# Loading two of six chunk rows with three large transfers in a one-core RWKV-and-MLP kernel

## The chip, the cores and the metric

The kernel runs on one core of one Trainium2 chip. The metric is the device time in microseconds of one execution. A core has TensorE (PE in the profile; PEld is its weight load), VectorE (DVE), ScalarE (ACT), GpSimd (POOL) and SyncE (SP), each with an instruction queue of its own that is worked off in order, and 16 DMA engines that carry out transfers which SP or ACT issue (SPq, ACTq).

## What is computed

The inputs r, k and v are fp32 of shape batch 4, heads 8, sequence 768, head width 48. A linear recurrence over the sequence is followed by a layer norm without offset and a two-layer MLP with a residual:

```python
for t in range(S):
    cur = np.einsum('bhd,bhe->bhde', u[None] * kt, vt)
    y[:, :, t] = np.einsum('bhd,bhde->bhe', rt, state + cur)
    state = w[None, :, :, None] * state + np.einsum('bhd,bhe->bhde', kt, vt)
...
xn = (x - mu) / np.sqrt(var + 1e-06) * g_ln      # x: (4, 768, 384), the heads side by side
ch = np.maximum(xn @ w_ch1, 0.0) @ w_ch2         # 384 -> 1536 -> 384
return (x + ch).astype(np.float32)
```

## The kernel before

The sequence is cut into six chunks of 128 tokens. With four batches that makes 24 tiles; tile i is chunk i // 4 of batch i % 4, with the 128 tokens on the partitions and 8 x 48 values along each partition. "Chunk rows 3 and 6" of the change are chunks 2 and 5 when counted from zero: tiles 8 to 11 and 20 to 23.

A tile goes through these steps, each a small function that a plan calls by a short name:

- LR, LK and LV (L325, L322, L328) load r, k and v of the tile, 192 KiB each, by a DMA that SP issues. One row of such a load is 48 fp32 values, 192 bytes.
- SR and SK (L334, L331) scale r and k by powers of the decay into the bf16 tile sc, through the helper of L194. CV (L337) casts v to bf16 (vv), through the helper copy of L187 to L191.
- r and k are turned so that the head width lies on the partitions: for the first eight tiles by PE (TR, TCr, TCk, TC), from tile 8 on by TKR (L489), a DMA transpose from sc to trs that SP issues.
- AT (L359) multiplies turned k and r, AM (L387) masks the product in PSUM into A, Q (L356) and S (L390) make the current-token term and the state update, CC copies the former to cc, ZU and ZD update the state Z, VB (L426) multiplies v by cc, Y (L432) multiplies by the state and by v, and X (L451) adds both into x.
- SQ and RS make the norm's factor, XN (L463) centres x into xn, and LT, LT2 or LTD turn it into xT. LT2 (L482) is a DMA transpose for two tiles at a time, issued by SP.
- UP (L511) multiplies xT by the first weight matrix into the PSUM pool hp, which has two buffers; RL (L528) applies the relu into hT and so frees the buffer; DN (L540) multiplies by the second matrix; OT (L602) adds the residual, and STO (L609) stores the tile.

The order of everything is written out by hand. PLAN (L18 to L67) is a list of steps "name,index,engine" with v for DVE, s for ACT, g for POOL; the loop of L619 calls them in that order, and each engine's queue, SP's too, gets its instructions in the order in which the plan names them. All r, k and v loads, all DMA transposes, the six weight loads and most stores are in SP's one queue. The stretch of the plan that matters for the prediction has LR,8 at the end of its line 31, and then these lines of the file:

```
32: Y,5,- CC,5,s RL,64,s DN,8,- LK,8,- AM,6,v VB,5,g TR,7,- RS,2,g LK,9,- UP,65,- UP,66,- Q,6,v TC,7,s X,5,v ZU,5,v DN,9,-
33: CV,7,g LV,8,- RL,66,s CV,6,g AT,7,- SQ,3,s RS,4,g XN,5,v LV,9,- Q,7,v S,6,- SR,8,v LT,5,- LR,10,- DN,10,- ZU,6,v SK,8,g
34: CC,6,s SQ,5,s RL,65,s XT,5,v Y,6,- STO,0,s AM,7,v S,7,- UP,81,- VB,6,g TKR,8,- LK,10,- SK,9,g OT,2,v UP,80,- CC,7,v X,6,v
35: SR,9,g DN,16,- RL,80,v XN,6,s Y,7,- CV,8,s RS,5,g DN,17,- VB,7,v TKR,9,- RL,81,s STO,1,- X,7,v CV,9,g DN,18,- ZU,7,v SQ,7,s
36: XN,7,g UP,82,- OT,4,v Q,8,g LT2,6,- AT,8,- RL,82,s DN,20,- LK,11,- AM,8,v LR,11,- SK,10,g S,8,- DN,21,- CC,8,s RS,3,g Y,8,-
```

Loaded tiles live in rings (L118 to L125): kf, rf and vf have 11 buffers each, and a load into a buffer waits until the readers of the tile 11 places earlier are done. Beside that, an SP transfer waits for the landing of the one eight places before it on the same completion counter, so about eight are under way at most.

Of the kernel before, what the change touches and what calls it, by code (L numbers as in the profile page):

```python
# [7 lines left out]
FP32 = mybir.dt.float32  # L8
# [5 lines left out]
GROUPS = [1, 1, 1, 1, 1, 1, 2, 2, 2, 2, 2, 2, 2, 1, 1, 1, 1]  # L14
ZPE = [4, 5, 6, 7]
K_BY_DMA = [8, 9, 10, 11, 12, 13, 14, 15, 16, 17, 18, 19, 20, 21, 22, 23]
SLOTS = {'kf': 11, 'rf': 11, 'vf': 11, 'sc': 3, 'vv': 4, 'trs': 3, 'q': 2, 'A': 2, 'cc': 4, 'Z': 6, 'ZS': 2, 'Vb': 3, 'x': 13, 'xn': 4, 'xT': 4, 'hT': 4, 'ot': 4}
PLAN = """  # L18
MP,0,v LR,1,- WF,0,s MW,0,v MI,0,g LR,0,- MM,0,g TL,0,s LC,1,- LK,0,- LV,0,- LN,0,s FR,0,s LC,0,s LR,2,- LK,1,- LC,2,s
SR,0,v FK,0,s SK,0,v LK,3,- DU,40,- CT,0,- TR,0,- CV,0,v LK,2,- SR,1,v TCr,0,s CP,0,v TCk,0,v UW,0,g LV,1,- UGC,0,s WL,0,s  # L20
# [50 lines left out]
def kernel(  # L71
# [12 lines left out]
    nc = tc.nc  # L84
    P = nc.NUM_PARTITIONS
    B, H, S, D = r.shape
    C = H * D
    L = P
    NCH = S // L
    NT = B * NCH  # L90
# [12 lines left out]
    const = ctx.enter_context(tc.tile_pool(name="const", bufs=1))  # L103
# [14 lines left out]
    def ring(name, shape, dtype):  # L118
        n = SLOTS[name]
        tiles = [const.tile(shape, dtype, name=f"{name}{a}") for a in range(n)]  # L120
        return lambda i: tiles[i % n]

    kf = ring("kf", [P, H, D], FP32)
    rf = ring("rf", [P, H, D], FP32)
    vf = ring("vf", [P, H, D], FP32)  # L125
    sc = ring("sc", [P, 2, H, DP], BF16)
    vv = ring("vv", [P, H, D], BF16)
    trs = ring("trs", [P, 2, HP, P], BF16)
    qq = ring("q", [P, HP, P], BF16)
    AA = ring("A", [P, 2, HP, P], BF16)  # L130
    cc = ring("cc", [P, H], FP32)
    ZZ = ring("Z", [P, HP, E2], BF16)
    ZS = ring("ZS", [P, HP, E2], FP32)
    Vb = ring("Vb", [P, C], FP32)
    xx = ring("x", [P, C], FP32)
    xn2 = [const.tile([P, 2, C], BF16, name=f"xn{a}") for a in range(SLOTS["xn"] // 2)]
    xT = ring("xT", [P, GM, CK, P], BF16)
    hT = ring("hT", [P, FK, GM * P], BF16)
    ot2 = [const.tile([P, 2, C], FP32, name=f"ot{a}") for a in range(SLOTS["ot"] // 2)]

    def scr(i):
        return sc(i)[:, 0]

    def sck(i):
        return sc(i)[:, 1]
# [17 lines left out]
    Fr = const.tile([P, H, D], FP32, name="Fr")  # L163
    Fk = const.tile([P, H, D], FP32, name="Fk")
# [3 lines left out]
    rows = const.tile([NR, P], FP32, name="rows")  # L168
# [18 lines left out]
    def copy(e, out, in_):  # L187
        if e == "s":
            nc.scalar.copy(out=out, in_=in_)  # L189
        else:  # L190
            engines[e].tensor_copy(out=out, in_=in_)  # L191

    def times(e, out, in0, in1):
        engines[e].tensor_tensor(out=out, in0=in0, in1=in1, op=ALU.mult)  # L194
# [4 lines left out]
    def chunk_src(t, i):  # L199
        c, b = divmod(i, B)  # L200
        return t[b, :, c * L : (c + 1) * L, :].rearrange("h t d -> t h d")
# [47 lines left out]
    def MP(i, e):  # L249
        for a in range(SLOTS["sc"]):  # L250
            nc.vector.memset(sc(a)[:, :, :, D:DP], 0.0)
        nc.vector.memset(WLZ[:], 0.0)
        nc.vector.memset(uwI[:], 0.0)
        nc.vector.memset(expo[:], -0.5)
# [56 lines left out]
    def w2_f(n):  # L311
        return w1_f[n][:].rearrange("p k f -> p (k f)").rearrange("p (a c) -> p a c", c=C)
# [4 lines left out]
    def CW(i, e):  # L317
        n, a = divmod(i, 2)
        h = FK // NW // 2
        copy(e, w2_sb[n][:, a * h : (a + 1) * h, :], w2_f(n)[:, a * h : (a + 1) * h, :])  # L320

    def LK(i, e):  # L322
        nc.sync.dma_start(out=kf(i)[:], in_=chunk_src(k, i))  # L323

    def LR(i, e):  # L325
        nc.sync.dma_start(out=rf(i)[:], in_=chunk_src(r, i))  # L326

    def LV(i, e):  # L328
        nc.sync.dma_start(out=vf(i)[:], in_=chunk_src(v, i))  # L329

    def SK(i, e):  # L331
        times(e, sck(i)[:, :, :D], kf(i)[:], Fk[:])

    def SR(i, e):  # L334
        times(e, scr(i)[:, :, :D], rf(i)[:], Fr[:])

    def CV(i, e):  # L337
        copy(e, vv(i)[:], vf(i)[:])

    def TR(i, e):  # L340
        t = psum["tr", i] = ps.tile([P, 2 * HP, P], BF16, name="tr")
# [83 lines left out]

    def VB(i, e):  # L426
        engines[e].tensor_tensor(  # L427
            out=Vb(i)[:].rearrange("p (h d) -> p h d", h=H), in0=vf(i)[:],
            in1=cc(i)[:].unsqueeze(2).to_broadcast([P, H, D]), op=ALU.mult,
        )  # L430

# [177 lines left out]
    def STO(i, e):  # L609
# [3 lines left out]
    steps = dict(  # L613
        WF=WF, LC=LC, CT=CT, CP=CP, LT2=LT2, TKR=TKR, DU=DU, MW=MW, TL=TL, MI=MI, MM=MM, MP=MP, WU=WU, LN=LN, FK=FK_, FR=FR_, UGC=UGC,
        UW=UW, WL=WL, LW1=LW1, SW=SW, LW2=LW2, CW=CW, LK=LK, LR=LR, LV=LV, SK=SK, SR=SR, CV=CV, TR=TR, TCr=TCr,
        TCk=TCk, TC=TC, Q=Q, AT=AT, AMa=AMa, AMb=AMb, AM=AM, S=S_, CC=CC, ZU=ZU, ZD=ZD, VB=VB, Y=Y, X=X,
        SQ=SQ, XN=XN, RS=RS, LT=LT, LTD=LTD, TKD=TKD, TRD=TRD, XT=XT, UP=UP, RL=RL, DN=DN, OT=OT, STO=STO, DA=DA, DB=DB, OA=OA, OB=OB, SA=SA, SB=SB,
    )
    for step in PLAN.split():  # L619
        name, i, e = step.split(",")  # L620
# [31 lines left out]
```

## Time and profile before

| what | value |
|---|---|
| median of three runs (lowest to highest) | 156.37 us (155.73 to 157.08) |
| span of the profiled execution | 156.2 us; what lies around it is taken as the 0.15 us to the median |
| PE busy | 139.4 us (89%) |
| DVE, ACT, POOL busy | 112.9, 75.1, 87.9 us (72%, 48%, 56%) |
| DMA packets, bytes | 104465, 30.03 MB |
| granted PE clock | 1.00 in every stretch |

The page gives, for one profiled execution, the busy time of each engine, the span in 40 equal slices (a digit is the busy share in tenths), the DMA queues, the chain of work that ended last, the costliest groups of instructions and the DMA issues. Other views of the same trace list single stretches: the timeline of one engine (start, duration, engine, line, operation, output <- inputs, count, and in square brackets the idle time before it and what ended it) and a table of windows (busy microseconds of each engine, granted clock, mean busy share of the 16 DMA engines and the rate in GB/s). The DMA share can pass 1, since packets of one engine overlap.

### The profile page before, as it was taken

What the parts mean: (1) busy time and instruction counts of PE and PEld (TensorE: products, weight loads), DVE (VectorE), ACT (ScalarE), POOL (GpSimd) and SP (SyncE); (2) the same over time, 40 slices, a digit from 0 to 9 for tenths busy, and PEclk for the clock granted to TensorE, in tenths of its full rate; (3) what the DMA queues carried; (4) which work ended last, traced back from release to release, by engine and by line L of the source; (5) the groups of instructions that cost most, each with busy time, mean ns of one, the idle gap of its engine ahead of it and who ended that gap; (6) DMA issues with size and microseconds to landing.
All of it is one profiled execution on the core that took longest, in us unless ns stands there. A gap on an engine that the chain in (4) does not pass through costs nothing.

```text
span 156.2 us, 4227 instructions
## 1 busy us (share of the span) xinstructions
PE 139.4 (89%) x1676; PEld 106.5 (68%) x1676; DVE 112.9 (72%) x224; ACT 75.1 (48%) x167; POOL 87.9 (56%) x127
## 2 busy tenths in 40 slices
PE   5659998999999869969969989998997999979991
PEld 1146687886778558757947767786775777758881
DVE  2149899996989856957659998899786767644421
ACT  3424666993766317135736547344253446615130
POOL 3016596503889979639739885134929885651000
PEclk9999999999999999999999999999999999999999
DMA  4999999988999979989989999999999898831221
GB/s 86 201 211 274 265 310 254 408 171 164 203 191 189 235 142 241 162 186 234 176 196 228 225 175 203 176 215 175 213 217 183 200 221 181 186 110 54 76 84 67
DMA packets 104465, 30.03 MB, mean 192 GB/s; under 512 B 99579, under 2 KB 102910, under 8 KB 104446
## 3 DMA queue, kind: packets, MB, share of 16 engines
q1 hardware_dynamic: 103132, 28.09, 89.4%
q10 hardware_dynamic: 1314, 1.67, 3.4%
q8 instruction: 13, 0.21, 0.6%
q14 instruction: 6, 0.05, 0.1%
HBM read 19.08 MB, written 4.72 MB: 152 GB/s over the span
## 4 chain that ended last, share of the span: by engine, by line
PE 29%; DMA 26%; SPq 21%; DVE 9%; POOL 5%; issue 4%; ACT 4%; ACTq 1%; DVEq 0%; POOLq 0%
PE hp L520 10%; PE o L548 9%; DMA xT<-xn 8%; DMA rf<-in_r_dram 8%; SPq L326 7%; SPq L329 5%; SPq L323 4%; DMA out_dram<-ot 3%; DMA w_all<-in_w_dram 2%; DMA kf<-in_k_dram 2%; DVE A L374 2%; POOL sc L194 2%; PE at L364 2%; PE o L261 2%; PE y L445 1%
## 5 line engine op out<-in xcount | busy, mean ns | idle before, releaser
L520 PE MATMUL hp<-xT,w_sb 128*128 128x128 bf16 (+1 forms) x612 | 57.1, 241 | 3.5 <-DMA xT<-xn 3.4
L548 PE MATMUL o<-w_sb,hT 128*128 128x384 bf16 x276 | 55.4, 326 | 0.6 <-DVE ot L604 0.4
L520 PEld LDWEIGHTS <-w_sb 128*128 128x128 bf16 x612 | 48.7, 114 | 8.4 <-DMA xT<-xn 3.2
L536 ACT ACTIVATE hT<-hp 128x512 bf16<-128x512 f32 x54 | 31.6, 595 | 34.4 <-PE hp L520 34.2
L548 PEld LDWEIGHTS <-hT 128*128 128x128 bf16 x276 | 24.2, 97 | 12.0 <-issue 0.8
L374 DVE TENSOR_TENSOR A<-at,mask 128x1024 bf16<-128x1024 f32 (+1 forms) x27 | 29.5, 1099 | 2.4 <-PE at L364 2.3
L194 POOL TENSOR_TENSOR sc<-kf,Fk 128x384 bf16<-128x384 f32 x15 | 15.4, 1026 | 14.9 <-DMA kf<-in_k_dram 9.0
L194 POOL TENSOR_TENSOR sc<-rf,Fr 128x384 bf16<-128x384 f32 x15 | 15.5, 1035 | 12.2 <-DMA rf<-in_r_dram 12.2
L604 DVE SCALAR_TENSOR_TENSOR ot<-o,rs,x 128x384 f32<-128x384 f32 x23 | 14.1, 614 | 8.7 <-PE o L548 4.3
L452 DVE SCALAR_TENSOR_TENSOR x<-y,Vb 128x384 f32<-128x384 f32 x24 | 13.2, 551 | 4.2 <-PE y L445 2.8
L427 POOL TENSOR_TENSOR Vb<-vf,cc 128x384 f32<-128x384 f32 x15 | 12.8, 850 | 6.0 <-DVE cc L191 4.3
L459 ACT ACTIVATE sqj<-x,sm 128x384 bf16<-128x384 f32 x24 | 14.7, 613 | 1.9 <-DVE x L452 1.8
L538 DVE TENSOR_SCALAR hT<-hp 128x512 bf16<-128x512 f32 x18 | 12.3, 686 | 3.1 <-PE hp L520 2.8
L364 PE MATMUL at<-trs 48*128 48x128 bf16 x192 | 10.0, 226 | 3.0 <-DMA trs<-sc 2.5
L476 POOL TENSOR_TENSOR rs<-rs,expo 128x1 f32<-128x1 f32 (+1 forms) x17 | 11.0, 649 | 1.4
L364 PEld LDWEIGHTS <-trs 48*128 48x128 bf16 x192 | 5.6, 97 | 8.6 <-DMA trs<-sc 3.9
L261 PE MATMUL o<-warm 128*128 128x512 bf16 x23 | 9.4, 533 | 2.0 <-DVE warm L226 2.0
L189 ACT CAST vv<-vf 128x384 bf16<-128x384 f32 x13 | 6.6, 509 | 9.2 <-DMA vf<-in_v_dram 7.8
L194 DVE TENSOR_TENSOR q<-trs 128x512 bf16<-128x512 bf16 x16 | 8.9, 555 | 2.6 <-DMA trs<-sc 2.5
L189 ACT COPY trs<-tr 128x512 bf16<-128x512 bf16 (+1 forms) x8 | 5.9, 747 | 9.3 <-PE tr L345 7.6
L194 POOL TENSOR_TENSOR q<-trs 128x512 bf16<-128x512 bf16 x8 | 9.6, 1196 | 0.9 <-PE hp L520 0.8
L445 PE MATMUL y<-vv,A 128*128 128x48 bf16 x192 | 8.8, 185 | 0.6 <-ACT vv L189 0.4
(76 smaller groups left out, 168.2 us busy)
## 6 DMA issues: line engine op xcount, KB each, us to landing
rf<-in_r_dram SPq DMA_DIRECT2D x24, 192.0 KB, 3.6
kf<-in_k_dram SPq DMA_DIRECT2D x24, 192.0 KB, 4.0
vf<-in_v_dram SPq DMA_DIRECT2D x24, 192.0 KB, 4.3
w_f<-in_moe_w_ch_dram SPq DMA_DIRECT2D x6, 768.0 KB, 6.1
out_dram<-ot SPq DMA_DIRECT2D x16, 192.0 KB, 3.6
out_dram<-ot ACTq DMA_DIRECT2D x7, 192.0 KB, 3.6
trs<-sc SPq DMA_TRANSPOSE x16, 3.5
w_all<-in_w_dram ACTq DMA_DIRECT2D x1, 192.0 KB, 3.8
```

Of the source, the lines that this page charges most:

```text
L189: nc.scalar.copy(out=out, in_=in_)
L194: engines[e].tensor_tensor(out=out, in0=in0, in1=in1, op=ALU.mult)
L261: nc.tensor.matmul(out=warm_ps[0][:], lhsT=warm[:], rhs=warm[:].unsqueeze(1).to_broadcast([P, 4, P]), start=True, stop=True)
L364: nc.tensor.matmul(out=t[:, par, q, :], lhsT=trs(i)[p0 : p0 + D, 1, q, :], rhs=trs(i)[p0 : p0 + D, 0, q, :], start=True, stop=True,)
L374: nc.vector.tensor_tensor(out=AA(i)[:, a:b].rearrange("p e q t -> p (e q) t"), in0=psum["at", i][:, a:b].rearrange("p e q t -> p (e q) t") ...
L427: engines[e].tensor_tensor(out=Vb(i)[:].rearrange("p (h d) -> p h d", h=H), in0=vf(i)[:], in1=cc(i)[:].unsqueeze(2).to_broadcast([P, H, D] ...
L452: nc.vector.scalar_tensor_tensor(out=xx(i)[:], in0=psum["y", i][:, :C], scalar=1.0, in1=Vb(i)[:], op0=ALU.mult, op1=ALU.add, accum_out=sm[ ...
L459: nc.scalar.activation(out=sqj[:], in_=xx(i)[:], func=ACT.Square, bias=sm[i][:], scale=-float(C), accum_out=sq[g][:, j : j + 1])
L520: nc.tensor.matmul(out=t[:, a * gw : (a + 1) * gw].rearrange("p (j t) -> p j t", j=size), lhsT=w1_sb[n][kc][:, fb::FB], rhs=xT(g)[:, :size ...
L536: nc.scalar.activation(out=o, in_=s, func=ACT.Relu)
L548: nc.tensor.matmul(out=psum["o", i][:, :C], lhsT=hT(g)[:, fk, j * P : (j + 1) * P], rhs=w2_sb[d][:, a, :], start=(fk == 0), stop=(fk == FK ...
L604: nc.vector.scalar_tensor_tensor(out=ot(i), in0=psum["o", i][:, :C], scalar=rs[g][:, j : j + 1], in1=xx(i)[:], op0=ALU.mult, op1=ALU.add,)
```

## The change

The loads of tiles 8 to 11 and 20 to 23 go into three tiles of their own, k_pair, r_pair and v_pair, which hold both chunk rows of all four batches. LR,8, LK,8 and LV,8 each issue one transfer of 1.5 MiB; LR, LK and LV of the other seven of these tiles issue nothing. The plan is not changed. Each transfer names 64 rows of 192 bytes for each of 128 tokens; four neighbouring tokens are adjacent in memory, and the built instruction reads 768 bytes at a time (32 groups of tokens x 64 rows x 192 values) and writes four rows of 192 bytes to four partitions. In k_pair the rows are 256 bytes apart, in the other two 192. The rings kf, rf and vf shrink to 6 buffers and serve the 16 remaining tiles. SK, SR, CV and VB of the eight tiles read from the new tiles, with a step between rows.

```diff
+PAIRED = [2, 5]
-SLOTS = {'kf': 11, 'rf': 11, 'vf': 11, 'sc': 3, ...
+SLOTS = {'kf': 6, 'rf': 6, 'vf': 6, 'sc': 3, ...
...
+    DW = 64
+    k_pair = const.tile([P, B, H, 2, DW], FP32, name="k_pair")
+    r_pair = const.tile([P, B, H, 2, D], FP32, name="r_pair")
+    v_pair = const.tile([P, B, H, 2, D], FP32, name="v_pair")
+
+    singles = [i for i in range(NT) if i // B not in PAIRED]
+
+    def rows_of(i, rings, pair):
+        c, b = divmod(i, B)
+        if c in PAIRED:
+            return pair[:, b, :, PAIRED.index(c), :D]
+        return rings(singles.index(i))[:]
...
+    def load(i, t, rows, pair):
+        c0, c1 = PAIRED
+        if i // B not in PAIRED:
+            nc.sync.dma_start(out=rows, in_=chunk_src(t, i))
+        elif i == c0 * B:
+            whole = t.rearrange("b h (c p) d -> p (b h c) d", p=L)
+            nc.sync.dma_start(
+                out=pair[:].rearrange("p b h c d -> p (b h c) d")[:, :, :D], in_=whole[:, c0 :: c1 - c0, :]
+            )
+
     def LK(i, e):
-        nc.sync.dma_start(out=kf(i)[:], in_=chunk_src(k, i))
+        load(i, k, kf(i), k_pair)
```

LR and LV are changed like LK, and SK, SR, CV and VB take kf(i), rf(i) and vf(i) without the index.

In SP's queue the 24 loads become three. Where the kernel before has LR,8, LR,9, LK,8, LK,9, LV,8, LV,9, LR,10, TKR,8, LK,10, TKR,9, STO,1, LT2,6, the changed one has r_pair, k_pair, v_pair, TKR,8, TKR,9, STO,1, LT2,6. The queues of PE, DVE, ACT and POOL hold the same instructions in the same order.

More of the change, by code (lines that the diff above doesn't have):

```diff
@@ L16 @@
 K_BY_DMA = [8, 9, 10, 11, 12, 13, 14, 15, 16, 17, 18, 19, 20, 21, 22, 23]
-SLOTS = {'kf': 11, 'rf': 11, 'vf': 11, 'sc': 3, 'vv': 4, 'trs': 3, 'q': 2, 'A': 2, 'cc': 4, 'Z': 6, 'ZS': 2, 'Vb': 3, 'x': 13, 'xn': 4, 'xT': 4, 'hT': 4, 'ot': 4}
+PAIRED = [2, 5]
+SLOTS = {'kf': 6, 'rf': 6, 'vf': 6, 'sc': 3, 'vv': 4, 'trs': 3, 'q': 2, 'A': 2, 'cc': 4, 'Z': 6, 'ZS': 2, 'Vb': 3, 'x': 13, 'xn': 4, 'xT': 4, 'hT': 4, 'ot': 4}
 PLAN = """
@@ L121, in ring, with kf, rf, vf @@
         return lambda i: tiles[i % n]
-    kf = ring("kf", [P, H, D], FP32)
-    rf = ring("rf", [P, H, D], FP32)
-    vf = ring("vf", [P, H, D], FP32)
+    kf_ring = ring("kf", [P, H, D], FP32)
+    rf_ring = ring("rf", [P, H, D], FP32)
+    vf_ring = ring("vf", [P, H, D], FP32)
+    DW = 64
[8 more added lines that the diff above has]
+        return rings(singles.index(i))[:]
+    def kf(i):
+        return rows_of(i, kf_ring, k_pair)
+    def rf(i):
+        return rows_of(i, rf_ring, r_pair)
+    def vf(i):
+        return rows_of(i, vf_ring, v_pair)
     sc = ring("sc", [P, 2, H, DP], BF16)
@@ L320, in CW @@
         copy(e, w2_sb[n][:, a * h : (a + 1) * h, :], w2_f(n)[:, a * h : (a + 1) * h, :])
+    def load(i, t, rows, pair):
[7 more added lines that the diff above has]
+            )
     def LK(i, e):
-        nc.sync.dma_start(out=kf(i)[:], in_=chunk_src(k, i))
+        load(i, k, kf(i), k_pair)
     def LR(i, e):
-        nc.sync.dma_start(out=rf(i)[:], in_=chunk_src(r, i))
+        load(i, r, rf(i), r_pair)
     def LV(i, e):
-        nc.sync.dma_start(out=vf(i)[:], in_=chunk_src(v, i))
+        load(i, v, vf(i), v_pair)
     def SK(i, e):
-        times(e, sck(i)[:, :, :D], kf(i)[:], Fk[:])
+        times(e, sck(i)[:, :, :D], kf(i), Fk[:])
     def SR(i, e):
-        times(e, scr(i)[:, :, :D], rf(i)[:], Fr[:])
+        times(e, scr(i)[:, :, :D], rf(i), Fr[:])
     def CV(i, e):
-        copy(e, vv(i)[:], vf(i)[:])
+        copy(e, vv(i)[:], vf(i))
     def TR(i, e):
@@ L427, in VB @@
         engines[e].tensor_tensor(
-            out=Vb(i)[:].rearrange("p (h d) -> p h d", h=H), in0=vf(i)[:],
+            out=Vb(i)[:].rearrange("p (h d) -> p h d", h=H), in0=vf(i),
             in1=cc(i)[:].unsqueeze(2).to_broadcast([P, H, D]), op=ALU.mult,
```

## The prediction

> **What bounds the kernel now.** I read the page first, then the table of windows, then the timelines of SP, POOL, ACT and PE around the place of the change.
>
> ```profile
> span 156.2 us, 4227 instructions
> PE 139.4 (89%) x1676; PEld 106.5 (68%) x1676; DVE 112.9 (72%) x224; ACT 75.1 (48%) x167; POOL 87.9 (56%) x127
> ...
> DMA  4999999988999979989989999999999898831221
> ...
> DMA packets 104465, 30.03 MB, mean 192 GB/s; under 512 B 99579, under 2 KB 102910, under 8 KB 104446
> ...
> PE 29%; DMA 26%; SPq 21%; DVE 9%; POOL 5%; issue 4%; ACT 4%; ACTq 1%; DVEq 0%; POOLq 0%
> ...
> rf<-in_r_dram SPq DMA_DIRECT2D x24, 192.0 KB, 3.6
> ```
>
> Two resources are nearly full. PE is busy 139.4 of 156.2 us. The DMA engines stand at eight or nine tenths from the second slice to about 130 us, and almost all packets (99579 of 104465) are under 512 bytes: the 192-byte rows of r, k and v and the small pieces of the transposes. The chain that ended last changes between PE, DMA and SP's queue, so neither alone sets the time. The next view says what the DMA engines deliver, by kind of transfer.
>
> ```profile
> core 0: us, PE busy (x) PEld busy (x) DVE busy (x) ACT busy (x) POOL busy (x), PEclk, DMA share, GB/s
> 40.00:46.00 6.00, 6.00 (x96) 4.50 (x94) 5.55 (x12) 4.45 (x10) 5.12 (x10) 1.00 1.01 200
> 28.50:31.50 3.00, 3.00 (x55) 2.48 (x54) 3.00 (x6) 2.82 (x6) 1.09 (x2) 1.00 1.01 402
> 153.50:155.50 2.00, 0.00 (x0) 0.00 (x0) 0.08 (x1) 0.00 (x0) 0.00 (x0) 1.00 0.29 98
> 56.00:144.00 88.00, 80.77 (x931) 62.85 (x930) 66.69 (x123) 41.12 (x99) 55.82 (x73) 1.00 1.00 190
> ```
>
> From 40 to 46 us only 192-byte loads move, the share is 1.01 and the rate 200 GB/s: the engines are full, and this is what they make of such rows. From 28.5 to 31.5 us the second weight matrix moves in long rows, also at a full share, at 402 GB/s. The two half stores at the end have rows of 768 bytes: 98 GB/s at a share of 0.29 is 338 GB/s at a full one. The last row gives PE's slack behind the place of the change: 88.00 - 80.77 = 7.23 us idle between 56 and 144.
>
> Now the place itself, in SP's queue and in the engines that read the new tiles:
>
> ```profile
> start us, us, engine line op out<-in xcount [idle before <-releaser]
> 38.56 1.15 SPq L329 DMA_DIRECT2D vf<-in_v_dram  x1
> 39.76 1.56 SPq L326 DMA_DIRECT2D rf<-in_r_dram  x2
> 41.36 2.11 SPq L323 DMA_DIRECT2D kf<-in_k_dram  x2
> 43.52 2.42 SPq L329 DMA_DIRECT2D vf<-in_v_dram  x2
> 45.99 0.63 SPq L326 DMA_DIRECT2D rf<-in_r_dram  x1
> 47.30 1.94 SPq L490 DMA_TRANSPOSE trs<-sc  x1
> 49.30 0.57 SPq L323 DMA_DIRECT2D kf<-in_k_dram  x1
> 50.04 1.87 SPq L490 DMA_TRANSPOSE trs<-sc  x1
> 51.95 0.58 SPq L611 DMA_DIRECT2D out_dram<-ot  x1
> 52.65 1.31 SPq L484 DMA_TRANSPOSE xT<-xn  x1
> ```
>
> LR,8 and LR,9 are issued from 39.76 us on, TKR,8 (the first DMA transpose) at 47.30, TKR,9 at 50.04 and LT2,6 at 52.65.
>
> ```profile
> 46.28 1.00 POOL L194 TENSOR_TENSOR sc<-kf,Fk 128x384 bf16<-128x384 f32 x1 [0.33 <-PE tr L505]
> 51.06 0.51 POOL L191 CAST vv<-vf 128x384 bf16<-128x384 f32 x1
> 51.68 0.59 POOL L467 TENSOR_SCALAR xn<-x,sm 128x384 bf16<-128x384 f32 x1
> 52.30 1.16 POOL L194 TENSOR_TENSOR q<-trs 128x512 bf16<-128x512 bf16 x1
> ```
>
> ```profile
> 49.57 0.50 ACT L189 CAST vv<-vf 128x384 bf16<-128x384 f32 x1
> 49.98 0.59 ACT L536 ACTIVATE hT<-hp 128x512 bf16<-128x512 f32 x1
> ```
>
> ```profile
> 51.08 0.83 PE L520 MATMUL hp<-xT,w_sb 128*128 128x128 bf16 x12
> 52.28 0.40 PE L364 MATMUL at<-trs 48*128 48x128 bf16 x8 [0.37 <-DMA trs<-sc]
> 57.25 1.47 PE L520 MATMUL hp<-xT,w_sb 128*128 128x256 bf16 x12 [1.18 <-DMA xT<-xn]
> 68.58 0.85 PE L520 MATMUL hp<-xT,w_sb 128*128 128x256 bf16 x6 [1.18 <-DMA xT<-xn]
> 80.47 0.40 PE L364 MATMUL at<-trs 48*128 48x128 bf16 x8 [1.20 <-DMA trs<-sc]
> 119.14 0.40 PE L364 MATMUL at<-trs 48*128 48x128 bf16 x8 [0.98 <-DMA trs<-sc]
> ```
>
> By the plan these are: SK,8 on POOL at 46.28, CV,9, XN,7 and Q,8 from 51.06; CV,8 and RL,81 on ACT at 49.57 and 49.98; UP,82, AT,8 and UP,97 on PE at 51.08, 52.28 and 57.25. Tile 8 has no reserve: PE reaches AT,8 and waits 0.37 us for TKR,8.
>
> **The change, part by part.** *The burst.* Before, tiles 8 and 9 bring 6 x 192 KiB = 1.2 MB ahead of TKR,8. Now 3 x 1.5 MiB = 4.72 MB are queued there, the rows of tiles 10, 11 and 20 to 23 among them, and the last third to come is v. The price is 4.72 MB over a rate that the trace of before does not show for this transfer: 768-byte reads with 192-byte writes. Bounds: 200 GB/s, if the write of each row sets the pace (7.86 us per transfer), and 338 to 402 GB/s, if the reads do (4.65 to 3.9 us). I take 200, because the written rows are the very rows of that window, still 8192 in each transfer; only the reads get longer. The padding of k could free k alone; that is a rival below.
>
> *When v is there.* LR,8 is issued at 39.76 and a load lands 3.6 us later, so its 0.197 MB are there at 43.4 us, with everything queued earlier ahead of it. r_pair stands at the same place. The other 4.52 MB take 22.6 us at 200 GB/s: v_pair lands at 43.4 + 22.6 = 66.0 us.
>
> *Who waits for it.* Three queues stand still, each with other work behind the waiting step. ACT has CV,8 ahead of RL,81; RL,81 frees the first of two hp buffers, and PE's UP,82 needs it. POOL has CV,9 ahead of XN,7 and Q,8, and before that SK,8 waits for k_pair. In SP's queue TKR,8, TKR,9 and LT2,6 come behind v_pair, so their packets come after its packets. DVE stands at SR,8 until r_pair lands and later at X,6, whose VB,6 is behind SK,8 on POOL. So PE idles in pieces before UP,82, and the last of them ends with v. UP,82 then starts at 66.0 + 0.50 (CV,8) + 0.59 (RL,81) = 67.1, against 51.08. From there to UP,97 before took 57.25 - 51.08 = 6.17 us, with waits of 0.37 and 1.18 in it: 4.6 us of work. TKR,8 (two microseconds behind v at the earliest) and LT2,6 (issued once XN,7 is done, 1.1 us after v) come out at about the same place. UP,97 starts at 67.1 + 4.6 = 71.7: 14.4 us late. Should the transposes pass v_pair in the queue, ACT and POOL would still hold PE, so I give this nothing.
>
> *What comes back.* From there on 18 of the 72 loads are already done (tiles 10 and 11 and 20 to 23, three each), and the transposes and stores find a shorter queue. The waits of PE that a DMA ended, at 68.58, 80.47 and 119.14, are 1.18 + 1.20 + 0.98 = 3.4 us; I take all three back. The upper bound is all of PE's slack behind UP,97, 7.23 - 1.18 = 6.05 us; the lower is nothing.
>
> *A cold PE.* The trace has PE after a long pause only at the start:
>
> ```profile
> 1.95 4.45 PE L261 MATMUL o<-warm 128*128 128x512 bf16 x10 [1.95 <-DVE warm L226]
> ...
> 19.06 1.24 PE L261 MATMUL o<-warm 128*128 128x512 bf16 x5
> ```
>
> The same matmul takes 445 ns at the start and about half of that (five in 1.24 us) at 19 us, though the granted clock stands at 1.00 throughout. If the pause before v costs such a slow stretch again, 4.45 us of work at half speed are 2.2 us too many; waits of 1.2 us left no mark. Between 0 and 2.2 I take 1.0. The Trainium skill, "TensorE: Matmul & The Clock Gate", section "What's actually happening", says that PE's clock is halved after an idle window of some 3.4 us and comes back after as long a busy one; by that rule the term would be an estimated 1.7 us, and the sum 0.7 us more.
>
> *Small parts, costed together.* 21 issues of about 0.6 us leave SP's queue; SP waits at the transposes anyway. The rings of 6 hold nothing up: tile 18 takes the place of tile 12 and tile 12 that of tile 2, whose readers stand far ahead in the plan. SK, SR, CV and VB read rows with a step; their element counts are the same, and POOL and ACT have 44% and 52% free. If a stepped read cost a quarter more, that would be 0.25 us on each of some 30 instructions that mostly have room.
>
> *The sum* against the profiled span: 156.2 + 14.4 - 3.4 + 1.0 = 168.2; with the 0.15 us to the median, 168.4 us.
>
> **The rivals.** *The reads gain in part.* If k alone does, since it is padded (338 GB/s, r and v at 200), the burst ends 7.86 - 4.65 = 3.2 us earlier: 165.2 us. If all three go halfway between 200 and 338, at 269 GB/s, v lands at 60.2 us and UP,97 is 8.7 us late: 156.4 + 8.7 - 3.4 + 1.0 = 162.7 us. For it speaks that longer rows are faster in every window (200, 338, 402 GB/s); against it that those windows have long rows on both sides. The Trainium skill, "DMA: Bandwidth & Descriptors", section "Why small descriptors are slow (HBM only)", gives each packet a fixed three cycles beside one for each 32 bytes. By that rule four packets of 192 bytes cost 36 cycles and one of 768 bytes 27, an estimated 267 GB/s and about the second of these times; the windows agree in direction, and no run so far shows what the short writes then do.
>
> *The reads set the pace, and the DMA relief decides: faster.* At the 402 GB/s of the long rows v lands at 43.4 + 11.2 = 54.6, UP,97 starts 3.0 us late, and with all 6.05 us of slack recovered the time is 156.4 - 3.0 = 153.4 us. It decides where the delay equals what comes back: v before 57.6 us, 318 GB/s. For it speaks the full DMA share up to 130 us; against it that the written rows stay at 192 bytes.
>
> *The same pace as the half stores*, 338 GB/s: v at 56.8, 5.2 us late, 3.4 to 6.05 back: 155.6 to 158.2 us, no measurable change or nearly.
>
> *The burst is slower than single loads.* If each read that feeds four partitions costs more, say 160 GB/s, v lands at 71.7 and the time is 174.1 us. Nothing in the trace speaks for it, since it has no such transfer.
>
> *The wide read doesn't come about.* Then 200 GB/s holds all the same, and the time is that of the forecast; only the packet count tells.
>
> **How the numbers follow.** The forecast has 0.60 (166 to 171 us), a partial gain in the reads 0.22 (161 to 166), the slower burst 0.08, the pace of the half stores 0.06, the faster one 0.04. The predicted time is that of the likeliest case, 168.4 us. The range of 161 to 173 leaves out the last three in the main. Within 1% of 156.37 us (154.8 to 157.9) is about what a measurement of this kernel can't tell from no change: faster 0.04, the same 0.06, slower 0.90.
>
> **What would show it.** In the changed profile the three transfers should end one after another at about 50, 58 and 66 us, at a rate near 200 GB/s; UP,82 should start right behind CV,8 and RL,81 on ACT at 67 us, and UP,97 at about 72; PE's later waits for trs and xT should be gone, and the packets should fall by 24576 - 6144 = 18432 to about 86000 if the reads are wide. The prediction is wrong if the burst runs well over 250 GB/s, if PE has other work in the pause than the plan's order gives it, or if the DMA waits behind it were not the DMA engines' load.

## The result and the profile after

| | before | changed |
|---|---|---|
| median of four runs each (lowest to highest) | 156.05 us (154.57 to 157.08) | 169.72 us (169.23 to 171.5) |
| span of the profiled execution | 156.2 us | 167.4 us (its own time 169.23 us) |
| ratio to the kernel before, 95% interval | | 1.095 (1.085 to 1.104) |

The change makes the kernel slower by 9.5%. Ratios here and below are made from fast runs alone: a run more than 1.5% above the fastest of its kernel is left out. The page of the changed kernel:

```profile
span 167.4 us, 4200 instructions
PE 140.9 (84%) x1676; PEld 107.6 (64%) x1676; DVE 112.6 (67%) x224; ACT 75.1 (45%) x167; POOL 88.4 (53%) x127
...
PE   5569999999906327889999779899989999999992
...
PEclk9975999999996957999999999999999999999999
DMA  4999999979999999994599999899793761631212
...
DMA packets 85697, 30.03 MB, mean 179 GB/s; under 512 B 74667, under 2 KB 84142, under 8 KB 85678
```

The packets fell by 18768, about the 18432 that wide reads should save: the reads are wide. All the same the DMA row is full from the second slice to the 18th, but for one. PE's row has a hole in slices 12 to 16, from 46 to 67 us, and PE's clock falls in the same slices (13, 15 and 16), beside two at the start. The place itself, first in SP's queue, then on the engines that read the new tiles:

```profile
39.10 0.84 SPq L350 DMA_DIRECT2D r_pair<-in_r_dram  x1
40.39 7.07 SPq L350 DMA_DIRECT2D k_pair<-in_k_dram  x1
47.91 9.00 SPq L350 DMA_DIRECT2D v_pair<-in_v_dram  x1
60.38 6.66 SPq L522 DMA_TRANSPOSE trs<-sc  x2
67.09 0.57 SPq L643 DMA_DIRECT2D out_dram<-ot  x1
67.78 1.23 SPq L516 DMA_TRANSPOSE xT<-xn  x1
```

```profile
50.42 0.56 DVE L216 TENSOR_TENSOR sc<-r_pair,Fr 128x384 bf16<-128x384 f32 x1 [6.10 <-DMA r_pair<-in_r_dram]
...
61.17 0.56 DVE L484 SCALAR_TENSOR_TENSOR x<-y,Vb 128x384 f32<-128x384 f32 x1 [7.73 <-POOL Vb L459]
...
61.65 0.69 DVE L570 TENSOR_SCALAR hT<-hp 128x512 bf16<-128x512 f32 x1
```

```profile
59.35 0.99 POOL L216 TENSOR_TENSOR sc<-k_pair,Fk 128x384 bf16<-128x384 f32 x1 [14.34 <-DMA k_pair<-in_k_dram]
...
66.49 0.50 POOL L213 CAST vv<-v_pair 128x384 bf16<-128x384 f32 x1 [2.34 <-DMA v_pair<-in_v_dram]
67.11 0.59 POOL L499 TENSOR_SCALAR xn<-x,sm 128x384 bf16<-128x384 f32 x1
```

```profile
66.46 0.51 ACT L211 CAST vv<-v_pair 128x384 bf16<-128x384 f32 x1 [4.07 <-DMA v_pair<-in_v_dram]
66.88 0.59 ACT L568 ACTIVATE hT<-hp 128x512 bf16<-128x512 f32 x1
```

The brackets name the three transfers one after the other: DVE waits for r until 50.4 us, POOL for k until 59.4, and ACT and POOL for v until 66.5. SP takes on the two transposes at 60.38, once POOL has scaled k, and behind v_pair; it holds them 6.7 us, until v is there. PE, and the rates in the windows of each transfer (the last three figures of a row are the granted clock, the DMA share and GB/s):

```profile
51.70 0.25 PE L427 MATMUL s<-uwI,q 128*128 128x2 bf16 x4 [5.31 <-ACT cc L211]
61.79 0.50 PE L469 MATMUL y<-Z,trs 128*128 128x96 bf16 x4 [6.08 <-DVE x L484]
...
64.97 0.88 PE L552 MATMUL hp<-xT,w_sb 128*128 128x128 bf16 x12
67.52 0.40 PE L396 MATMUL at<-trs 48*128 48x128 bf16 x8 [1.67 <-DMA trs<-sc]
...
72.01 1.47 PE L552 MATMUL hp<-xT,w_sb 128*128 128x256 bf16 x12 [0.59 <-DMA xT<-xn]
82.34 0.84 PE L552 MATMUL hp<-xT,w_sb 128*128 128x256 bf16 x6 [0.17 <-DMA xT<-xn]
94.29 0.40 PE L396 MATMUL at<-trs 48*128 48x128 bf16 x8 [1.23 <-DMA trs<-sc]
```

```profile
43.00:46.00 3.00, 3.00 (x45) 2.12 (x43) 1.32 (x3) 1.59 (x4) 1.84 (x5) 1.00 1.09 219
50.00:57.00 7.00, 4.02 (x37) 3.33 (x36) 3.02 (x6) 1.26 (x4) 0.00 (x0) 0.76 1.11 163
60.00:65.00 5.00, 3.21 (x21) 1.87 (x22) 3.33 (x7) 0.62 (x1) 3.98 (x6) 0.50 1.09 219
```

PE's one long pause is three waits of 5.3, 6.1 and 1.7 us, one for each transfer, with a little work between; UP,97 starts at 72.01, 14.8 us later than before. From there to the end the changed kernel takes 167.4 - 72.0 = 95.4 us, the kernel before 156.2 - 57.25 = 99.0: between these two executions 3.6 us are given back. r and v moved at 219 GB/s, and k, the tensor with the padded rows, at 163.

### The profile page after: what moved, and what is told of

The parts are those of the page before. It is cut to its first block, busy times and chain, and to the rows that moved or that the text cites. A ratio compares the mean times of both kernels' runs of the same rounds, so it can differ in the third digit from the quotient of the medians.

```text
span 167.4 us, 4200 instructions
## 1 busy us (share of the span) xinstructions
PE 140.9 (84%) x1676; PEld 107.6 (64%) x1676; DVE 112.6 (67%) x224; ACT 75.1 (45%) x167; POOL 88.4 (53%) x127
## 3 DMA queue, kind: packets, MB, share of 16 engines
HBM read 19.08 MB, written 4.72 MB: 142 GB/s over the span
## 4 chain that ended last, share of the span: by engine, by line
PE 40%; DMA 22%; SPq 15%; POOL 8%; DVE 6%; ACT 3%; issue 3%; ACTq 1%; DVEq 0%; POOLq 0%
PE o L580 15%; PE hp L552 15%; DMA v_pair<-in_v_dram 11%; SPq L347 9%; SPq L350 5%; DMA out_dram<-ot 3%; DMA xT<-xn 3%; POOL sc L216 2%; DMA w_all<-in_w_dram 2%; POOL q L216 2%; PE at L396 2%; DMA kf<-in_k_dram 2%; PE y L477 2%; PE o L283 1%; DVE A L406 1%
## 5 line engine op out<-in xcount | busy, mean ns | idle before, releaser
L580 PE MATMUL o<-w_sb,hT 128*128 128x384 bf16 x276 | 56.6, 332 | 2.0 <-DVE ot L636 1.4
L552 PEld LDWEIGHTS <-w_sb 128*128 128x128 bf16 x612 | 50.1, 115 | 5.5 <-issue 1.1
L216 POOL TENSOR_TENSOR sc<-kf,Fk 128x384 bf16<-128x384 f32 x9 | 9.0, 1004 | 11.4 <-DMA kf<-in_k_dram 5.5
L216 POOL TENSOR_TENSOR sc<-rf,Fr 128x384 bf16<-128x384 f32 x9 | 9.5, 1054 | 8.9 <-DMA rf<-in_r_dram 8.9
L216 POOL TENSOR_TENSOR sc<-k_pair,Fk 128x384 bf16<-128x384 f32 x6 | 6.3, 1053 | 14.3 <-DMA k_pair<-in_k_dram 14.3
L497 ACT ACTIVATE xn<-x,sm 128x384 bf16<-128x384 f32 x11 | 6.7, 612 | 12.1 <-DVE x L484 12.1
L469 PE MATMUL y<-Z,trs 128*128 128x96 bf16 x80 | 6.9, 210 | 6.1 <-DVE x L484 6.1
L427 PE MATMUL s<-uwI,q 128*128 128x2 bf16 x96 | 5.9, 166 | 6.0 <-ACT cc L211 5.3
L427 PEld LDWEIGHTS <-q 128*128 128x128 bf16 x96 | 5.4, 99 | 8.3 <-issue 5.4
L469 PEld LDWEIGHTS <-trs 128*128 128x128 bf16 x80 | 5.4, 99 | 8.1 <-DVE x L484 6.5
```

The source lines that it names most:

```text
L469: nc.tensor.matmul(out=t[:, q * E2 : (q + 1) * E2], lhsT=trs(i)[:, 0, q, :], rhs=ZZ(i - B)[:, q, :], start=first, stop=True, skip_group_ch ...
L552: nc.tensor.matmul(out=t[:, a * gw : (a + 1) * gw].rearrange("p (j t) -> p j t", j=size), lhsT=w1_sb[n][kc][:, fb::FB], rhs=xT(g)[:, :size ...
L580: nc.tensor.matmul(out=psum["o", i][:, :C], lhsT=hT(g)[:, fk, j * P : (j + 1) * P], rhs=w2_sb[d][:, a, :], start=(fk == 0), stop=(fk == FK ...
```

## The experiments

The theory: the time is lost because 4.72 MB stand in SP's queue and in the DMA engines ahead of what tile 8 needs; PE resumes when the last of them has landed, and the rate is set by the 192-byte writes. The rivals: the padding or the place in the queue sets k's rate; the size of one transfer, the stepped reads or the smaller rings cost something by themselves.

**k without padding.**

```diff
-    DW = 64
+    DW = 48
```

> k_pair with rows of 192 bytes side by side, like r_pair and v_pair. In the changed kernel k_pair's packets ran from 48.56 to 58.33 us (9.8 us) where r_pair's and v_pair's took 7.7. Theory: the padding itself slows the writes, and the delay follows the landing of v one to one; k_pair then takes 7.7 us, v lands 2 us earlier, and the time falls from 169.7 to about 167.7 us (ratio to the kernel before 1.08). Rival: the second of three transfers is slow for another reason (what moves beside it); k_pair stays at 9.8 us and the time at 169.7.

Ratio 1.079 (1.070 to 1.089). k_pair now moves like the others, in the window from 52 to 56 us:

```profile
52.00:56.00 4.00, 3.30 (x34) 3.13 (x34) 2.44 (x5) 1.26 (x4) 0.00 (x0) 0.50 1.10 219
```

The padding costs: 163 GB/s with it, 219 without. The ratio is 1.5% lower, 2.4 us of 156, where 2 were expected; the two intervals overlap, so the size of the gain is less certain than the rate. In the profiled execution UP,97 is no earlier (72.11 us), because r_pair was issued 0.9 us later than in the changed kernel's; but from the landing of r to that of k it took 58.59 - 51.42 = 7.2 us, against 59.35 - 50.42 = 8.9 with padding.

**The padding moved to v.**

```diff
+    k_pair = const.tile([P, B, H, 2, D], FP32, name="k_pair")
+    v_pair = const.tile([P, B, H, 2, DW], FP32, name="v_pair")
```

> The 256-byte rows moved from k_pair to v_pair. If padding slows a transfer, k_pair takes 7.7 us and v_pair 9.8, v lands where it did, and the time stays within 0.5 us of the changed kernel's 169.7, though k lands 2 us earlier. If the place as second in the queue is what is slow, k_pair stays at 9.8 us and v_pair at 7.7. If padding helps, as the edit would suggest, v_pair is under 7.7 us and the time under 168.

Ratio 1.087 (1.076 to 1.098), an interval that includes the 1.095 of the changed kernel but is too wide to test the half microsecond that was expected. From the profile, whose execution took 175.04 us, only the rates are read. The slow window went with the padding, from k (51 to 55 us) to v (60 to 66 us):

```profile
51.00:55.00 4.00, 1.56 (x18) 1.39 (x18) 2.84 (x5) 1.26 (x4) 0.00 (x0) 0.62 1.10 226
60.00:66.00 6.00, 3.73 (x32) 2.55 (x32) 3.85 (x8) 0.61 (x1) 3.33 (x5) 0.69 1.11 163
```

The place in the queue is not the cause.

**k rows 224 bytes apart** (DW = 56).

> k_pair with rows 224 bytes apart instead of 256. At 192 bytes (rows side by side) a transfer of 1.5 MiB took 7.6 us, at 256 it took 9.8 us. If a gap between the written rows is what slows, k_pair takes about 9.8 us again; if the 256-byte step is, it takes 7.6 to 7.8.

```profile
53.00:58.00 5.00, 3.52 (x33) 3.00 (x31) 1.36 (x3) 0.66 (x3) 0.00 (x0) 0.75 1.11 200
```

200 GB/s, or 7.9 us for 1.5 MiB if the whole transfer goes at that rate: between the two expectations, and nearer to the second. A step of 224 bytes costs 9% of the rate and one of 256 bytes a quarter (219, 200, 163 GB/s). Its time was 170.73 us, from a single run. Why a step of 256 bytes is slow, these runs don't tell; that it isn't the gap as such, the runs of single loads and half bursts show below.

**24 single loads at the same places.**

```diff
         elif i == c0 * B:
-            whole = t.rearrange("b h (c p) d -> p (b h c) d", p=L)
...
+            for c in PAIRED:
+                for b in range(B):
+                    nc.sync.dma_start(out=pair[:, b, :, PAIRED.index(c), :D], in_=chunk_src(t, c * B + b))
```

> The same 4.72 MB at the same three places of SP's queue, but as 24 transfers of 192 KiB with 192-byte reads, tile 8 first in each group of eight. Theory: what costs is that 4.72 MB stand in SP's queue ahead of the DMA transpose of tile 8, at 200 GB/s whatever the size of a read; the transpose lands at about 67 us, and the time is that of an unpadded burst, 167 to 168.5 us. Rival one: the landing of the large transfer as a whole is what holds ACT and POOL; here v of tile 8 lands about 7 us before the last of v, and the time falls to about 161. Rival two: wide reads save DMA time after all; then this is slower than the changed kernel, over 171.

Ratio 1.104 (1.095 to 1.112), 173.85 us against 157.64 us: above what the theory expected, and where the second rival had it. Its profile shows three differences, and none of them needs the narrow reads to be slow:

```profile
58.00 8.26 SPq L351 DMA_DIRECT2D v_pair<-in_v_dram  x8
66.43 2.99 SPq L521 DMA_TRANSPOSE trs<-sc  x2
```

```profile
70.37 0.61 PE L395 MATMUL at<-trs 48*128 48x128 bf16 x8 [10.23 <-DMA trs<-sc]
...
76.36 1.48 PE L551 MATMUL hp<-xT,w_sb 128*128 128x256 bf16 x12
```

```profile
53.00:60.00 7.00, 3.79 (x32) 2.51 (x32) 3.82 (x8) 0.61 (x1) 4.62 (x6) 0.56 1.50 166
62.00:66.00 4.00, 0.00 (x0) 0.00 (x0) 0.00 (x0) 2.09 (x5) 1.09 (x2) 0.58 1.13 201
```

First, k is still padded here, which the expectation overlooked. A single load fills every second row of a tile, so its rows are 512 bytes apart in k_pair, where they move at 166 GB/s (the padded wide reads had 163), and 384 bytes apart in v_pair, where they move at 201 GB/s against 219 for the wide reads. The half bursts below show that these 9% are not the reads'. Second, SP could issue the transposes only at 66.43, when the single loads ahead had been taken on, and AT,8 came 3.9 us after that. Third, PE was idle for 10.23 us in one piece. The first rival fell: tile 8's v was there when ACT cast it (63.11 us in this run's timeline), and PE still waited until 70.37 for the transpose behind the remaining loads. The queue is enough to hold PE without any large transfer.

```profile
63.11 0.51 ACT L211 CAST vv<-v_pair 128x384 bf16<-128x384 f32 x1 [6.30 <-DMA v_pair<-in_v_dram]
```

**24 single loads at their own places.**

```diff
-        if i // B not in PAIRED:
+        if i // B in PAIRED or i // B not in PAIRED:
             nc.sync.dma_start(out=rows, in_=chunk_src(t, i))
```

> The three tiles, the padded k rows, the stepped reads of SK, SR, CV and VB and the rings of 6 are kept, but each of the 24 loads is issued singly where the plan names it, as in the kernel before. Theory: all of the loss is the burst; the time is the 156 us of the kernel before, within 1.5 us. Rival: the stepped reads or the smaller rings cost something by themselves; over 158 us.

Ratio 0.999 (0.994 to 1.004). New tiles, padded k, stepped reads and rings of 6 together cost nothing that can be measured. So the loss is the burst's.

**Half the burst, twice and once.** In the first kernel (k not padded) each tensor has one transfer of 768 KiB for tiles 8 to 11 at tile 8's place and one for tiles 20 to 23 at tile 20's. The second keeps the former and loads tiles 20 to 23 singly. Each of these transfers reads 192 bytes at a time and writes rows 384 bytes apart. The edit of the first:

```diff
-        elif i == c0 * B:
-            whole = t.rearrange("b h (c p) d -> p (b h c) d", p=L)
+        elif i % B == 0:
+            j = PAIRED.index(i // B)
+            whole = t.rearrange("b h (c p) d -> p (b h) c d", p=L)
...
+                out=pair[:].rearrange("p b h c d -> p (b h) c d")[:, :, j, :D], in_=whole[:, :, i // B, :]
```

> The burst cut in two: at LR,8, LK,8 and LV,8 one transfer of 768 KiB per tensor for tiles 8 to 11, at LR,20, LK,20 and LV,20 one for tiles 20 to 23; k rows not padded, reads of 192 bytes. Theory: the delay follows the bytes that stand ahead of tile 8's DMA transpose. v of tiles 8 to 11 lands at 43.4 us + 2.16 MB at 200 GB/s = 54.2 us instead of 66, UP,97 comes about 3 us late instead of 14.4, and 6 loads rather than 18 are out of the way behind it: 1 us back. The second half stands ahead of late transposes and may cost again up to 3 us. Ratio to the kernel before 1.01 to 1.035. Rival: large transfers cost by their size as such; then two bursts cost together what one did, and the ratio stays near 1.08.

Ratio 1.059 (1.052 to 1.065), neither the theory's 1.01 to 1.035 nor the rival's 1.08. The first half did what was worked out: UP,97 at 59.73 us is 2.5 us late, where about 3 were expected. The rate while it moved was no lower than that of the wide reads, 229 against 219 GB/s:

```profile
40.00:46.00 6.00, 6.00 (x96) 4.66 (x96) 4.33 (x9) 3.79 (x9) 4.46 (x8) 1.00 1.24 229
```

So reading 768 bytes at a time gains nothing that shows, and rows 384 bytes apart are not slow. What came behind the second half had not been worked out:

```profile
59.73 1.47 PE L553 MATMUL hp<-xT,w_sb 128*128 128x256 bf16 x12 [0.37 <-DMA xT<-xn]
...
113.64 0.40 PE L397 MATMUL at<-trs 48*128 48x128 bf16 x8 [1.62 <-DMA trs<-sc]
116.37 0.33 PE L441 MATMUL s<-vv,sc 128*128 128x96 bf16 x4 [1.13 <-POOL vv L213]
121.83 1.44 PE L581 MATMUL o<-w_sb,hT 128*128 128x384 bf16 x4 [3.45 <-DVE ot L637]
```

PE has three waits within some 10 us of the second half, the longest of them for DVE, which waits for a store:

```profile
121.16 0.62 DVE L637 SCALAR_TENSOR_TENSOR ot<-o,rs,x 128x384 f32<-128x384 f32 x1 [3.55 <-DMA out_dram<-ot]
```

To tell whether the loss belongs to the second half:

> The first half burst alone: tiles 8 to 11 by one transfer of 768 KiB per tensor at LR,8, LK,8 and LV,8, tiles 20 to 23 loaded singly where the plan names them. In the run with two half bursts UP,97 came 2.5 us late, and 4 us more were lost behind it. Theory: those 4 us are the second half burst, by the same mechanism at the second place; without it the time is 1.5 to 3.5 us over the kernel before, ratio 1.01 to 1.022. Rival: the first half burst disturbs the rest of the run by itself; ratio 1.04 to 1.06.

Ratio 1.015 (1.007 to 1.023): as the theory had it. So the second half costs about 4.4%; its loss was underestimated, since stores stand behind it too.

**18 loads left out.** The kernel leaves out the loads of r, k and v of tiles 10, 11 and 20 to 23, which read tiles 8's and 9's values instead.

```diff
-            return pair[:, b, :, PAIRED.index(c), :D]
+            return pair[:, b % 2, :, 0, :D]
...
-        if i // B not in PAIRED:
+        if i // B not in PAIRED or i in (8, 9):
```

> Leaves out 18 loads, those of r, k and v of tiles 10, 11 and 20 to 23, which read the values of tiles 8 and 9 instead, so that the output is not the reference's; tiles 8 and 9 are loaded singly where the plan names them, and there is no burst. It prices what the burst gives back: the same 18 loads are missing behind the place of the change. Theory: PE's waits for DMA transposes behind that place go, 3.4 us, at most all of its idle time there, 6 us: ratio to the kernel before 0.96 to 0.98. Rival: the 3.5 us that the changed kernel made up came from engines that caught up while PE stood still; then leaving the loads out brings less than 1%, ratio over 0.99.

Ratio 0.989 (0.983 to 0.996), between the two. Having a quarter of all loads for nothing is worth 1.1%, or 1.7 us, less than half of the 3.6 us by which the two profiled executions differ behind UP,97. PE's wait at AT,13, which stands at 80.47 us before, is still there without the loads:

```profile
77.71 0.40 PE L391 MATMUL at<-trs 48*128 48x128 bf16 x8 [1.20 <-DMA trs<-sc]
```

So that wait is not the loads' doing; the prediction had named this as a sign of being wrong. Whether engines that caught up during the pause gave the rest was not measured; there may be no rest, as the paragraph on the sum below works out.

**PE kept busy in the pause.** The kernel with 24 single loads, with matmuls on zeros ahead of AT,8, whose result nobody reads.

```diff
-LT2,6,- AT,8,-
+LT2,6,- KW,30,- AT,8,-
```

> The kernel of the 24 single loads at one place, with 30 matmuls of 512 columns on zeros ahead of AT,8 on PE, where PE stood idle for 10.2 us; their result is read by nobody. In the run without them the granted clock was 0.50 from 64 to 76 us, so that PE's work from AT,8 on ran at half speed for some 6 us. Theory: the cold PE is a cost on the path; with the clock at 1.00 when AT,8 starts, 2 to 3 us come back, ratio 1.104 to about 1.085 to 1.09. Rival: PE waits for the other engines after the pause anyway, and its clock there costs nothing: ratio stays within 0.005 of 1.104.

Ratio 1.107 (1.101 to 1.112), no gain; but the condition wasn't met: the dummies ended 3.8 us early and the clock was at 0.54 from 70 to 72 us. Again with 48:

> As the run with 30 matmuls on zeros ahead of AT,8, but with 48, since the 30 ended 3.8 us before AT,8 and the clock had fallen to half again by then. They should now end within about a microsecond of AT,8, and the granted clock be 1.00 behind it. Theory: the cold PE costs 1 to 3 us on the path, ratio 1.085 to 1.098 against 1.104 without dummies. Rival: it costs nothing, since the other engines set the pace right after the pause; ratio 1.10 to 1.11 with the clock at 1.00.

Now the clock held. First the kernel with 48 dummies, then the one without:

```profile
72.00:74.00 2.00, 2.00 (x29) 1.61 (x26) 0.66 (x3) 0.03 (x1) 1.92 (x4) 1.00 0.32 65
```

```profile
72.00:74.00 2.00, 2.00 (x16) 1.16 (x14) 0.92 (x2) 0.17 (x1) 1.83 (x4) 0.50 0.15 19
```

```profile
69.49 0.40 PE L405 MATMUL at<-trs 48*128 48x128 bf16 x8 [1.45 <-DMA trs<-sc]
...
73.12 1.47 PE L561 MATMUL hp<-xT,w_sb 128*128 128x256 bf16 x12
```

From AT,8 to UP,97 PE takes 73.12 - 69.49 = 3.6 us, against 76.36 - 70.37 = 6.0 when cold: 2.4 us at that place. Over the whole run the ratio is 1.098 (1.092 to 1.105) against 1.104 (1.095 to 1.112): the intervals overlap, so how much of the 2.4 us (1.5%) reaches the end stays open; the two ratios differ by 0.5%. The Trainium skill, "TensorE: Matmul & The Clock Gate", section "What's actually happening", has the clock halved after a long idle window. The trace agrees as far as this goes, with 0.50 behind the pause of 10.2 us.

## Why the prediction was right, step by step

- *The rate, 200 GB/s.* The reason given, that the written rows set the pace and not the reads, holds: longer reads gained nothing (219 GB/s, against 229 with short reads in the half bursts), the step between the written rows cost a quarter (163). In detail the figure was wrong in both directions: r and v moved at 219, k at 163. That this comes out almost even over the three is luck: v was there for ACT at 66.46 us, predicted 66.0. The prediction had the padding as a possible gain for k. It was a loss, and without it the 200 would have been some 9% too low. The three transfers ended at 50, 59 and 66 us (predicted about 50, 58, 66).
- *Who waits.* CV,8 on ACT, CV,9 and XN,7 on POOL and TKR,8 in SP's queue all resumed with v, as said. One link was wrong: UP,82 doesn't need RL,81 on ACT. It ran at 64.97 us, before RL,81 at 66.88, and after DVE's relu at 61.65 (RL,80, which the plan names before RL,81). It didn't matter, because AT,8 waited for TKR,8 until 67.52 and LT2,6 was behind XN,7. TKR,8 let PE go on about one microsecond behind v (66.46 and 67.52 us), not two. UP,97 came at 72.01, predicted 71.7: 14.8 us late against 14.4.
- *What comes back, 3.4 us.* This step failed, though the spans give 3.6 us. Of the three waits named, 1.18, 1.20 and 0.98 us, the first shrank to 0.17 and the third went, but the second stayed at 1.23, and it stays without the 18 loads too. In its place two later waits of the kernel before went, and one of 0.92 us for DVE's ot came (97.68 us):

```profile
129.08 0.36 PE L445 MATMUL y<-vv,A 128*128 128x48 bf16 x8 [0.40 <-ACT vv L189]
139.32 0.86 PE L520 MATMUL hp<-xT,w_sb 128*128 128x128 bf16 x12 [1.06 <-DMA xT<-xn]
```

- *A cold PE, 1.0 us.* Nothing here. The clock did fall to 0.50 in the pause, but PE had Y,7, DN and UP,82 to do from 61.8 to 65.9 us while it waited for v anyway, and by AT,8 the profile shows 1.00 again. With one undivided pause, as in the run of single loads, 2.4 us appear at that place.
- *The sum.* 156.2 + 14.8 - 3.6 + 0 = 167.4 us is the span. The time around the span was taken as 0.15 us; the runs listed with both figures have 1.8 us (169.23 - 167.4). By that the profiled execution of before took 156.2 + 1.8 = 158.0 us, 1.6 us more than the median of 156.37, and the sum should have been made with 1.8 us around it. That, and the 1.0 us for the cold PE that was not paid, are the two terms that were mis-sized; that they partly cancel in 168.4 against 169.72 is luck. The medians tell the same 2 us in another way: 169.72 - 156.05 = 13.7 us were lost, so if UP,97 is 14.8 us late in every run, only 1.1 us come back. That is near the 1.7 us of the run without the 18 loads. Two profiled executions can't decide between 1.1 and 3.6.
- *The rivals.* The faster one and that of the half stores' pace needed 318 GB/s and more; the highest window of the burst has 219. By the rule of the Trainium skill ("DMA: Bandwidth & Descriptors", "Why small descriptors are slow (HBM only)"), four short reads made into one would give an estimated 267 GB/s. The trace doesn't agree: 219 for the wide reads, and 200 to 229 for narrow ones, so the reads don't set the pace.

No version that loads all its data beats the kernel before. Even with 18 loads left out there was only 1.1% to win, which speaks for the engines that PE waits for, and not the loads' total, as what is left there.

## What to carry to other kernels

A large transfer in an in-order DMA queue is paid by whatever small, urgent transfer stands next behind it, at the queue's rate: bytes put in front, over the rate of a full window, gave the time at which PE resumed to about half a microsecond, twice (4.72 MB and 2.36 MB), the first time with some luck in the rate. When the DMA engines are full, fetching early what is needed late moves the wait forward instead of hiding it, and what it frees later is worth little (1.7 us here for 18 loads). Follow each queue to the first instruction that waits, and then to what stands behind it; several chains that end on the same landing make a forecast robust against one wrong link.

## What the runs showed that was not expected

- The rate goes with the step between the written rows of 192 bytes, and not with the size of the gap. With wide reads it is 219 GB/s side by side, 200 at 224 bytes and 163 at 256. With narrow reads it is 201 to 229 at 384 bytes and 166 at 512. Why 256 and 512 are slow, no run here tells.
- Reading 768 bytes at a time instead of 192 raises the rate by nothing that shows while the writes stay at 192 bytes: 219 GB/s, against 229 for large transfers with narrow reads and 200 to 201 for loads of 192 KiB.
- PE's clock fell to 0.50 within the pauses of some 5 us, and came back in time where PE had 4 us of other work before the last wait, but not where the pause was one of 10.2 us.
